# Eight lent buffers for the transposed bands of block one, first conversions traced behind the bands' divisions, and low parts and divisions moved from GpSimd to VectorE

## Chip, cores and metric

The kernel runs on one core of a Trainium2 chip. The metric is the device time of one execution in microseconds, as the median of several runs. Engines go by the profile's names: PE is TensorE (PEld its weight loads), DVE is VectorE, ACT is ScalarE, POOL is GpSimd, SP is SyncE, which issues the DMAs.

## What is computed

Attention over 4 batches of 8 heads (576 positions, 64 dimensions), made of a coarse part (q, k and v averaged over groups of four positions, softmax attention, each result repeated four times) and a local part (each position sees the positions less than four away). Two feed-forward layers of width 512 to 2048 to 512 over the 2304 tokens follow.

```python
out_up = np.repeat(sm_attn(q_d, k_d, v_d), factor, axis=2)      # q_d, k_d, v_d: means over 4 positions
scores = np.where(np.abs(pos[:, None] - pos[None, :]) < factor, scale * q @ k.T, -1e9)
out_local = softmax(scores) @ v
x = (out_up + out_local).transpose(0, 2, 1, 3).reshape(2304, 512)
h = x @ w_in;   x = np.maximum(h, 0.0) ** 2 @ w_out              # layer one
h = x @ w_in2;  return (h * np.cos(h)) @ w_out2                  # layer two
```

The weights arrive as 64-bit floats (two 32-bit words an element, which the kernel reads as integers and puts together itself). Matmul operands are split in a high and a low part, and each product is the sum of high x high, high x low and low x high.

## The kernel before

**Blocks.** Layer one goes over five blocks of tokens (8, 7, 7, 7 and 7 windows of 64 tokens). In each block, for each of 16 pieces `f` of the width 2048, `stage_a` (L711) multiplies the block's input `xh`, `xl` by piece `f` of `w_in` (12 matmuls into one PSUM bank, tag `h`), `gelem1` (L735, L736, L723) applies relu and square on ACT and makes the high part `gh`, `low` (L729) makes the low part `gl` on DVE, and `stage_b1` (L794) multiplies by piece `f` of `w_out`, 12 matmuls. Until layer one's last block the bank of `stage_a` has one buffer, so a new piece waits until the relu has read the one before.

**Input of a block.** A task `window(w)` makes the local attention of 64 tokens: it adds the mask and the scores (L475, L485), takes the maximum on DVE (L359), and goes through `exps`: even windows of block one and all of block two (`apiece`) scale the maximum (L361) and take four exponentials with sums on ACT (L363); odd ones of block one subtract on DVE (L370), take one exponential (L374) and sum on DVE (L376). Then come the reciprocal of the sum (L496, L497), the division of the band `pr` by the sum (L498, POOL), four transposes on PE (L508), a copy to `pt` on ACT (L510), the product with v (L528), the addition of the coarse part (L544, DVE), and for each pair of windows the high part `xh` (L555, ACT) and the low part `xl` (L556, DVE). `pool(b)` sums groups of four positions (L346, L351, L353; `early_v` does it at L303 for the first batch), and `down(b, hp)` makes the coarse attention (L389 to L434), whose division (L400) is on POOL.

**Buffers in the head.** While `early[0]` holds, before the first matmul of layer one, the eight windows of block one are under way together. Their bands have eight buffers: four of `pr`, and two each lent by the tiles `gt` and `gl`. Their transposes have five: two of `pt` and three lent by the tile `gh`. `band_tile` hands them out and `band_done` takes them back once the product with v has been issued. `xh` and `xl` (pool `xp`) have two buffers each; block one uses one of each.

**Conversion of weights.** `conv1(f)` loads piece `f` of layer one (`raw`, 1 MB, two buffers, an SP DMA at L568) and calls `split`: ACT scales the upper words (L582), DVE clips (L584), shifts (L587) and joins the lower words (L589), ACT rounds to the high part `hi1[f]` (L596), and the low part follows (L604, two halves of 512 columns): on POOL while `early[0]` holds, else on DVE. The low halves are written to DRAM for the later blocks. `conv2(u)` does the same for the 16 pieces of layer two, from slot 18 on, one each three slots; its low parts are made on POOL (L599, and L683 for the sums of odd pieces).

**Order.** Tasks are generators: each round of a loop advances every task by one step, and the order in which they are traced is the priority. From it a scheduler lays out each engine's queue, taking what its own timeline holds ready. Engines run their queues in order. `behind(names)` ties an instruction behind the last one of that name on its engine; the names set before are `hi` (L723), `gl` (L729), `xh` (L555), `xl` (L556), `exp` (L363), `max` (L359), `pr` (L498), `relu` (L735), `pe`. The first loop runs while there are tasks and puts two `warm` matmuls on PE after each round in which PE got work. After it `early[0]` is false; pieces 3 to 15 are converted while block one is under way, and `now[0]` is the number of the slot (block x 16 + piece). `after_first` ties everything traced later behind the last `pe`, `xh`, `xl` and `pr` instruction of the head, one for each engine.

Of the kernel before, what the change touches and what calls it, by code (L numbers as in the profile page):

```python
# [8 lines left out]
F32 = mybir.dt.float32  # L9
# [9 lines left out]
P = 128  # L19
# [55 lines left out]
def kernel(  # L75
# [114 lines left out]

    lent = {"pr": ["pr"] * caps["pr"] + ['gt', 'gt', 'gl', 'gl'], "pt": ["pt"] * caps["pt"] + ['gh', 'gh', 'gh']}

    def band_tile(name, shape):
        while early[0] and not lent[name]:
            yield
        if not early[0]:
            yield from need(name)
        tag = lent[name].pop(0) if early[0] else name
        if tag == name:
            return tag, cm.tile(shape, F32, tag=name, name=name, bufs=caps[name])  # L200
        t = gp.tile([P, TMAX], F32R if tag in ("gh", "gl") else F32, tag=tag, name=name, bufs=3 if tag == "gh" else 2)
        n = shape[1] * shape[2]
        return tag, t.bitcast(F32)[:shape[0], :n].rearrange("p (a b) -> p a b", a=shape[1])
# [14 lines left out]
    whole = {}  # L218
    scored = set()
    xds = {}  # L220
    qk_used = {}
# [136 lines left out]
    def exps(bank, sv, mx, pr, scale, apiece):  # L358
        last["max"] = nc.vector.tensor_reduce(out=mx[:, 0], in_=sv, op=ALU.max, axis=AX.X).ins  # L359
        if apiece:  # L360
            nc.vector.tensor_scalar_mul(out=mx[:, 0], in0=mx[:, 0], scalar1=-scale)  # L361
            for i in range(sv.shape[1]):
                last["exp"] = nc.scalar.activation(  # L363
                    out=pr[:, i], in_=sv[:, i], func=AF.Exp, bias=mx[:, 0, i:i + 1], scale=scale,
                    accum_out=mx[:, 1, i:i + 1],
                ).ins
            done_a(bank)
            yield
            return
# [81 lines left out]
    def window(w):  # L451
# [39 lines left out]
        else:  # L491
# [5 lines left out]
        nc.vector.reciprocal(out=mx[:, 1], in_=mx[:, 1])  # L497
        last["pr"] = nc.gpsimd.tensor_tensor(  # L498
            out=prv, in0=prv, in1=mx[:, 1].unsqueeze(2).broadcast_to([P, HPAIR, n]), op=ALU.mult
        ).ins  # L500
        yield
        if not early[0]:
# [74 lines left out]
    def split(raw, hi, los=None, sums=None):  # L577
# [3 lines left out]
        with behind("hi", "xh", "exp"):  # L581
            nc.scalar.activation(out=xv, in_=top.bitcast(F32), func=AF.Prelu, scale=TOP_SCALE, alpha=TOP_ALPHA)  # L582
        with behind("gl", "xl"):
            nc.vector.tensor_scalar(  # L584
                out=xv, in0=xv, scalar1=TOP_MAX, scalar2=-TOP_MAX * TOP_ALPHA, op0=ALU.min, op1=ALU.max
            )
# [11 lines left out]
        if los is None:  # L598
            nc.gpsimd.tensor_tensor(out=xv, in0=xv, in1=hi.bitcast(F32), op=ALU.subtract)  # L599
        else:  # L600
# [9 lines left out]
    def conv1(f, after=0):  # L610
# [3 lines left out]
        yield  # L614
        while len(ready) < after or len(scored) < 4:
            yield
# [7 lines left out]
        for said in split(raw, hi1[f], ring):  # L624
            if said:
                done("raw")
            yield
        for k, lo in enumerate(los):
            nc.sync.dma_start(out=lo_d[f][:, k * DM:(k + 1) * DM], in_=lo.bitcast(F32))
            lo1[0, f, k] = lo  # L630
# [9 lines left out]
    def conv2(u):  # L640
# [41 lines left out]
        yield  # L682
        nc.gpsimd.tensor_tensor(out=total, in0=total, in1=top.bitcast(F32), op=ALU.subtract)  # L683
        yield
# [238 lines left out]
    tasks += [window(w) for w in range(W0[1])]  # L923
    tasks += [conv1(0), conv1(1, 3), conv1(2, 6)]
    junk = ps_a.tile([P, 512], F32, tag="a", name="ps_warm")
# [9 lines left out]
    warm(WARM0)  # L935
    while tasks:
        before = last.get("pe")
# [33 lines left out]
    def x2_stream(j):  # L971
# [10 lines left out]
        for c in range(0, NK, 2):  # L982
            yield
            cs = slice(c, c + 2)
            nc.scalar.activation(out=xh[:, cs], in_=xf[:, cs], func=AF.Copy)
            nc.vector.tensor_tensor(out=xl[:, cs], in0=xf[:, cs], in1=xh[:, cs].bitcast(F32), op=ALU.subtract)

# [199 lines left out]
```

## Time and profile before

| | |
|---|---|
| median of 3 runs | 933.74 us (933.18, 933.74, 938.19) |
| the profiled execution, its own time | 938.64 us |
| its span, first to last instruction | 936.6 us |
| PE busy, instructions | 913.4 us, 6886 |
| DVE busy | 638.6 us |
| ACT busy | 580.4 us |
| POOL busy | 108.6 us, 89 instructions |
| granted TensorE clock, mean | 0.989 of full speed |

The span is what the rows below divide up; the 2.0 us between it and the execution's own time lie around it. Busy times of different engines overlap. A matmul counts as busy from its start to a modelled end, so a busy PE can be at half the clock. In each row of a timeline the first two numbers are the start and the length in us; what stands in brackets is the idle time before and what ended it.

### The profile page before, as it was taken

How to read it: one execution, taken by the hardware profiler on the slowest of the kernel's cores; microseconds unless marked ns; L12 is line 12 of the kernel's file. 1: busy time of each engine (PE TensorE's matmuls, PEld its weight loads, DVE VectorE, ACT ScalarE, POOL GpSimd, SP SyncE). 2: the span in 40 equal slices, each digit the busy share in tenths (PEclk: the TensorE clock that was granted, in tenths of full speed). 3: DMA queues.
4: the chain of work that ended last, by engine and by line, in shares of the span. 5: the costliest groups of instructions: out<-in, count | busy, mean ns of one | idle time of the engine just before them, and what ended most of it. 6: DMA issues, size and time to landing. Idle time of an engine off the chain costs nothing.

```text
span 936.6 us, 17648 instructions
## 1 busy us (share of the span) xinstructions
PE 913.4 (98%) x6886; PEld 835.4 (89%) x6886; DVE 638.6 (68%) x1207; ACT 580.4 (62%) x1024; POOL 108.6 (12%) x89
## 2 busy tenths in 40 slices
PE   7889999999999999999999999999999999999997
PEld 5668777788888888898999999999999999999997
DVE  6779986664568644554531168888787888888786
ACT  4678674555465554554553368677777677777774
POOL 2331101024033231231210000000000000000000
PEclk9789999999999999999999999999999999999999
DMA  9779876865899756966888885565665665655672
GB/s 233 209 253 318 306 266 220 291 214 172 298 310 323 239 210 243 341 245 226 294 301 307 284 320 190 187 212 182 196 203 184 199 209 191 207 194 188 213 236 101
DMA packets 74223, 222.77 MB, mean 238 GB/s; under 512 B 8932, under 2 KB 14436, under 8 KB 69916
## 3 DMA queue, kind: packets, MB, share of 16 engines
q1 hardware_dynamic: 74140, 221.64, 70.5%
q8 instruction: 54, 0.88, 0.4%
q14 instruction: 29, 0.24, 0.1%
HBM read 180.72 MB, written 40.89 MB: 237 GB/s over the span
## 4 chain that ended last, share of the span: by engine, by line
PE 87%; DVE 5%; DMA 5%; ACT 2%; issue 1%; POOL 0%; DVEq 0%; POOLq 0%; ACTq 0%
PE ps_h L746 22%; PE ps_h L711 19%; PE acc L794 19%; PE acc L818 18%; DMA pl<-in_pool_v_dram 3%; DMA pl<-in_pool_qk_dram 2%; PE ps_a L528 1%; PE ps_warm L931 1%; PE ps_a L485 1%; PE ps_a L508 1%; PE ps_a L389 1%; PE ps_a L426 1%; PE ps_a L410 1%; PE acc L816 1%; PE ps_acc L528 1%; DVE mx L359 1%
## 5 line engine op out<-in xcount | busy, mean ns | idle before, releaser
L746 PE MATMUL ps_h<-x,w2hi 128*128 128x256 f32 x1152 | 159.9, 281 | 0.0
L746 PEld LDWEIGHTS ps_h<-x,w2hi 128*128 128x128 f32 x1152 | 146.6, 189 | 0.1
L729 DVE TENSOR_TENSOR gl<-gt,gh 128x448 fp32r<-128x448 f32 (+1 forms) x80 | 56.2, 703 | 131.2 <-ACT gh L723 67.4
L818 PE MATMUL acc<-bl,gh 128*128 128x256 f32 x504 | 140.5, 280 | 0.0
L711 PE MATMUL ps_h<-xh,w1hi 128*128 128x448 f32 (+1 forms) x320 | 122.4, 384 | 4.8 <-ACT gt L735 4.8
L711 PE MATMUL ps_h<-xl,w1hi 128*128 128x448 f32 (+1 forms) x320 | 120.3, 376 | 0.0
L794 PE MATMUL acc<-gl,w1hi 128*128 128x448 f32 (+1 forms) x320 | 120.0, 375 | 0.2 <-DVE gl L729 0.2
L794 PE MATMUL acc<-gh,w1hi 128*128 128x448 f32 (+1 forms) x320 | 111.2, 377 | 2.2 <-ACT gh L723 2.2
L735 ACT ACTIVATE gt<-ps_h 128x448 f32<-128x448 f32 (+1 forms) x80 | 44.4, 555 | 110.2 <-PE ps_h L711 109.9
L818 PEld LDWEIGHTS acc<-bl,gh 128*128 128x128 f32 x504 | 94.9, 188 | 0.0
L794 PE MATMUL acc<-gh,lo 128*128 128x448 f32 x256 | 94.5, 369 | 0.0
L786 DVE TENSOR_TENSOR gl<-g,gh 128x896 fp32r<-128x896 f32 x72 | 78.2, 1086 | 11.0 <-ACT gh L781 11.0
L818 PE MATMUL acc<-w2hi,gh 128*128 128x256 f32 x288 | 80.9, 281 | 0.0
L754 ACT ACTIVATE u<-ps_h,quarter 128x512 f32<-128x512 f32 x72 | 49.5, 687 | 49.9 <-PE ps_h L746 49.6
L818 PE MATMUL acc<-w2hi,gl 128*128 128x256 f32 x288 | 80.3, 281 | 0.0
L761 DVE SCALAR_TENSOR_TENSOR r<-u,ps_h 128x512 f32<-128x512 f32 x72 | 49.4, 686 | 39.6 <-ACT u L756 34.0
L781 ACT ACTIVATE gh<-g 128x896 fp32r<-128x896 f32 x72 | 68.1, 946 | 10.7 <-DVE g L779 10.6
L711 PEld LDWEIGHTS ps_h<-xh,w1hi 128*128 128x128 f32 x320 | 60.6, 189 | 13.7 <-ACT gt L735 5.6
L766 ACT ACTIVATE r<-r,half_pi 128x512 f32<-128x512 f32 x72 | 51.8, 720 | 33.9 <-DVE r L762 33.9
L746 PE MATMUL ps_h<-x,w2lo 128*128 128x256 f32 x432 | 68.7, 281 | 0.0
L794 PEld LDWEIGHTS acc<-gh,w1hi 128*128 128x128 f32 x320 | 59.6, 188 | 9.4 <-ACT gh L723 2.7
L711 PEld LDWEIGHTS ps_h<-xl,w1hi 128*128 128x128 f32 x320 | 60.7, 190 | 6.8
(145 smaller groups left out, 1963.3 us busy)
## 6 DMA issues: line engine op xcount, KB each, us to landing
bl<-wo_d SPq DMA_DIRECT2D x70, 896.0 KB
raw<-in_w_dram SPq DMA_DIRECT2D x32, 1024.0 KB
lo<-lo_d SPq DMA_DIRECT2D x128, 256.0 KB
qkw<-in_win_qk_dram SPq DMA_DIRECT2D x28, 268.0 KB
pl<-in_pool_qk_dram SPq DMA_DIRECT2D x24, 288.0 KB
wo_d<-raw SPq DMA_DIRECT2D x16, 384.0 KB
out_dram<-o SPq DMA_DIRECT2D x18, 256.0 KB
lo_d<-loa SPq DMA_DIRECT2D x16, 256.0 KB
```

Of the source, the lines that this page charges most:

```text
L528: last["pe"] = nc.tensor.matmul(avv[rows, hp], vw[:n, hp * P + a * D:hp * P + (a + 1) * D], pt[:n, hp, a * WQ:(a + 1) * WQ], start=True, s ...
L711: nc.tensor.matmul(h[:, :n], a[:, c * P:(c + 1) * P], x[:, c, :n], start=i == 0, stop=i == len(order) - 1)
L729: last["gl"] = nc.vector.tensor_tensor(out=gl, in0=gt, in1=gh.bitcast(F32), op=ALU.subtract).ins
L735: last["relu"] = nc.scalar.activation(out=gt, in_=h, func=AF.Relu).ins
L746: nc.tensor.matmul(h[:, s * TB:(s + 1) * TB], a[:, c * P:(c + 1) * P], x[:, c], start=i == 0, stop=i == len(order) - 1,)
L754: nc.scalar.activation(out=u, in_=h, func=AF.Identity, bias=quarter, scale=float(1.0 / (2 * math.pi)))
L761: nc.vector.scalar_tensor_tensor(out=r, in0=u, scalar=-PI2_HI, in1=hv, op0=ALU.mult, op1=ALU.add)
L766: nc.scalar.activation(out=r, in_=r, func=AF.Sin, bias=half_pi, scale=1.0)
L781: nc.scalar.activation(out=gh, in_=g[:, 1:], func=AF.Copy)
L786: nc.vector.tensor_tensor(out=gl, in0=g[:, 1:], in1=gh.bitcast(F32), op=ALU.subtract)
L794: nc.tensor.matmul(acc[d][:, :n], a, x, start=f == 0 and i == 0, stop=f == NF - 1 and i == 2)
L818: nc.tensor.matmul(o, a[:, x], b, start=opens and i == 0, stop=p == NP2 - 1 and i == 2 and (k % 2 == 1 or k == NPROD - 1),)
```

## The change

Five things are altered. (1) The transposed bands of block one have eight buffers, two of `pt` and six slices of a first tile of `xh` (four) and of `xl` (two); `gh` lends none. (2) The divisions L498 of all 36 windows go to DVE. (3) The first pieces' `conv1` waits in the trace until all eight bands are divided (`turned`), for pieces zero and one in place of a number of finished windows, and their DVE steps are tied behind the last division; piece two stops before its high part until the first `hi` has been traced, and the head's loop ends without it, so that its low part is made on DVE. (4) The exponentials of windows that are traced in slots 0 and 1 are tied behind `hi`. (5) The low parts of layer two's weights go from POOL to DVE, tied behind `gl`; and the first casts of layer two's input are tied behind `hi` and `gl`. In `after_first` the entry of `pr` is now one of DVE, and stands in the place of that of `xl`.

```diff
--- before.py
+++ after.py
@@ -188,7 +188,8 @@
             got.append(t)
         return got
 
-    lent = {"pr": ["pr"] * caps["pr"] + ['gt', 'gt', 'gl', 'gl'], "pt": ["pt"] * caps["pt"] + ['gh', 'gh', 'gh']}
+    lent = {"pr": ["pr"] * caps["pr"] + ['gt', 'gt', 'gl', 'gl'], "pt": ["pt"] * caps["pt"] + list(range(6))}
+    scratch = {}
 
     def band_tile(name, shape):
         while early[0] and not lent[name]:
@@ -196,6 +197,11 @@
         if not early[0]:
             yield from need(name)
         tag = lent[name].pop(0) if early[0] else name
+        if isinstance(tag, int):
+            x, k = ("xh", "xl")[tag // NK], tag % NK
+            if x not in scratch:
+                scratch[x] = xp.tile([P, NK, TMAX], F32R, tag=x, name="xs").bitcast(F32)
+            return tag, scratch[x][:shape[0], k].rearrange("p (a b) -> p a b", a=shape[1])
         if tag == name:
             return tag, cm.tile(shape, F32, tag=name, name=name, bufs=caps[name])
         t = gp.tile([P, TMAX], F32R if tag in ("gh", "gl") else F32, tag=tag, name=name, bufs=3 if tag == "gh" else 2)
@@ -217,6 +223,7 @@
     pooled = {}
     whole = {}
     scored = set()
+    turned = set()
     xds = {}
     qk_used = {}
     vp_used = {}
@@ -360,10 +367,11 @@
         if apiece:
             nc.vector.tensor_scalar_mul(out=mx[:, 0], in0=mx[:, 0], scalar1=-scale)
             for i in range(sv.shape[1]):
-                last["exp"] = nc.scalar.activation(
-                    out=pr[:, i], in_=sv[:, i], func=AF.Exp, bias=mx[:, 0, i:i + 1], scale=scale,
-                    accum_out=mx[:, 1, i:i + 1],
-                ).ins
+                with behind("hi") if 0 <= now[0] < 2 else nullcontext():
+                    last["exp"] = nc.scalar.activation(
+                        out=pr[:, i], in_=sv[:, i], func=AF.Exp, bias=mx[:, 0, i:i + 1], scale=scale,
+                        accum_out=mx[:, 1, i:i + 1],
+                    ).ins
             done_a(bank)
             yield
             return
@@ -495,9 +503,10 @@
         yield from exps(s, sv, mx, prv, SCALE, w % 2 == 0 if apart else w < W0[2])
         nc.vector.tensor_scalar_add(out=mx[:, 1], in0=mx[:, 1], scalar1=1e-9)
         nc.vector.reciprocal(out=mx[:, 1], in_=mx[:, 1])
-        last["pr"] = nc.gpsimd.tensor_tensor(
+        last["pr"] = nc.vector.tensor_tensor(
             out=prv, in0=prv, in1=mx[:, 1].unsqueeze(2).broadcast_to([P, HPAIR, n]), op=ALU.mult
         ).ins
+        turned.add(w)
         yield
         if not early[0]:
             yield
@@ -580,7 +589,7 @@
         xv = x.bitcast(F32)
         with behind("hi", "xh", "exp"):
             nc.scalar.activation(out=xv, in_=top.bitcast(F32), func=AF.Prelu, scale=TOP_SCALE, alpha=TOP_ALPHA)
-        with behind("gl", "xl"):
+        with behind("gl", "pr" if early[0] else "xl"):
             nc.vector.tensor_scalar(
                 out=xv, in0=xv, scalar1=TOP_MAX, scalar2=-TOP_MAX * TOP_ALPHA, op0=ALU.min, op1=ALU.max
             )
@@ -596,7 +605,8 @@
             nc.scalar.activation(out=hi, in_=xv, func=AF.Copy)
         yield
         if los is None:
-            nc.gpsimd.tensor_tensor(out=xv, in0=xv, in1=hi.bitcast(F32), op=ALU.subtract)
+            with behind("gl", "xl"):
+                nc.vector.tensor_tensor(out=xv, in0=xv, in1=hi.bitcast(F32), op=ALU.subtract)
         else:
             for k, lo in enumerate(los()):
                 cs = slice(k * DM, (k + 1) * DM)
@@ -612,7 +622,7 @@
         raw = load_raw(1, f)
         yield
         yield
-        while len(ready) < after or len(scored) < 4:
+        while len(ready) < after or early[0] and len(turned) < (8 if f == 0 else 8):
             yield
         hi1[f] = wp.tile([P, 2 * DM], F32R, tag=f"hi{f}", name=f"w1hi{f}")
         los = []
@@ -625,6 +635,8 @@
             if said:
                 done("raw")
             yield
+            while f == 2 and said and "hi" not in last:
+                yield
         for k, lo in enumerate(los):
             nc.sync.dma_start(out=lo_d[f][:, k * DM:(k + 1) * DM], in_=lo.bitcast(F32))
             lo1[0, f, k] = lo
@@ -680,7 +692,8 @@
         with behind("relu", "xh", "exp"):
             nc.scalar.activation(out=top, in_=total, func=AF.Copy)
         yield
-        nc.gpsimd.tensor_tensor(out=total, in0=total, in1=top.bitcast(F32), op=ALU.subtract)
+        with behind("gl", "xl"):
+            nc.vector.tensor_tensor(out=total, in0=total, in1=top.bitcast(F32), op=ALU.subtract)
         yield
         nc.sync.dma_start(out=wo_d[p][:, 2 * DM:m], in_=top.bitcast(F32))
         nc.sync.dma_start(out=wo_d[p][:, m + 2 * DM:], in_=total)
@@ -921,7 +934,7 @@
     tasks += [pool(0), early_v()]
     tasks += [down(0, hp) for hp in range(HPAIR)]
     tasks += [window(w) for w in range(W0[1])]
-    tasks += [conv1(0), conv1(1, 3), conv1(2, 6)]
+    tasks += [conv1(0, 0), conv1(1, 0), conv1(2, 6)]
     junk = ps_a.tile([P, 512], F32, tag="a", name="ps_warm")
     used["a"] += 1
 
@@ -933,7 +946,7 @@
                 )
 
     warm(WARM0)
-    while tasks:
+    while any(t.__name__ != "conv1" for t in tasks) or (0, 1, 1) not in lo1:
         before = last.get("pe")
         for t in list(tasks):
             if next(t, "end") == "end":
@@ -982,8 +995,10 @@
         for c in range(0, NK, 2):
             yield
             cs = slice(c, c + 2)
-            nc.scalar.activation(out=xh[:, cs], in_=xf[:, cs], func=AF.Copy)
-            nc.vector.tensor_tensor(out=xl[:, cs], in0=xf[:, cs], in1=xh[:, cs].bitcast(F32), op=ALU.subtract)
+            with behind("hi") if j == 0 else nullcontext():
+                nc.scalar.activation(out=xh[:, cs], in_=xf[:, cs], func=AF.Copy)
+            with behind("gl") if j == 0 else nullcontext():
+                nc.vector.tensor_tensor(out=xl[:, cs], in0=xf[:, cs], in1=xh[:, cs].bitcast(F32), op=ALU.subtract)
 
     n1 = NB * NF
     pend = []
```

## Rows read from the trace of the kernel before

**Rows 1.** The page: busy us of each engine, share, instructions.

```profile
PE 913.4 (98%) x6886; PEld 835.4 (89%) x6886; DVE 638.6 (68%) x1207; ACT 580.4 (62%) x1024; POOL 108.6 (12%) x89
```

**Rows 2.** Waits of PE, whole span: total us, times, longest.

```profile
PE ps_h L711 <- ACT gt L735: 4.8, 2, 4.6
```

**Rows 3.** Stretches: length, busy us of PE, PEld, DVE, ACT, POOL, clock, DMA.

```profile
13.20:25.50 12.30, 9.33 (x170) 7.62 (x168) 12.18 (x44) 9.99 (x56) 6.07 (x8) 1.00 0.96 205
...
40.00:48.60 8.60, 8.60 (x99) 7.13 (x99) 5.68 (x10) 4.65 (x8) 0.00 (x0) 0.50 0.20 61
...
51.80:56.30 4.50, 0.00 (x1) 0.01 (x1) 3.99 (x9) 3.04 (x18) 1.97 (x2) 0.91 0.74 266
56.30:65.10 8.80, 8.80 (x28) 7.04 (x29) 4.33 (x8) 6.21 (x10) 3.60 (x3) 0.66 0.70 242
65.10:163.00 97.90, 97.90 (x627) 77.04 (x626) 80.12 (x142) 69.16 (x161) 9.58 (x9) 1.00 0.80 274
163.00:176.00 13.00, 10.12 (x105) 7.90 (x105) 10.79 (x27) 6.27 (x13) 1.49 (x3) 1.00 0.73 236
```

**Rows 4.** The chain that ended last, 25 to 66 us: start, length, what.

```profile
25.62 4.50 DVE vp L303 x4
...
39.98 2.71 PE ps_acc L508 x12
...
43.54 2.76 PE ps_acc L528 x48
...
53.56 2.19 ACT pr L363 x14
```

**Rows 5.** Timeline of the head: DVE, POOL and ACT.

```profile
16.10 0.17 DVE L361 TENSOR_SCALAR dmx<-dmx 96x3 f32<-96x3 f32 x1
...
16.54 0.71 DVE L396 TENSOR_SCALAR dmx<-dmx 96x3 f32<-96x3 f32 x1
...
31.45 3.64 POOL L498 TENSOR_TENSOR pr<-pr,mx 128x280 f32<-128x280 f32 x3 [5.22 <-DVE mx L497]
...
32.75 1.21 DVE L589 SCALAR_TENSOR_TENSOR bits<-raw,bits 128x1024 uint32<-128x1024 uint32 x1
...
50.18 1.29 POOL L604 TENSOR_TENSOR loa<-bits,w1hi 128x512 fp32r<-128x512 f32 x1 [12.54 <-DVE kp L351]
...
51.94 1.29 DVE L361 TENSOR_SCALAR mx<-mx 128x4 f32<-128x4 f32 x2
...
55.61 0.63 ACT L735 ACTIVATE gt<-ps_h 128x512 f32<-128x512 f32 x1
```

**Rows 6.** Stretches, L711 alone: length, busy us of PE, PEld, clock, DMA.

```profile
48.50:51.80 3.30, 3.12 (x12) 2.17 (x12) 0.98 0.98 394
56.20:61.70 5.50, 5.40 (x12) 3.80 (x12) 0.50 0.72 275
```

**Rows 7.** Groups by shape, DVE, 13 to 34 us: busy us, mean ns, idle before.

```profile
L370 DVE TENSOR_TENSOR pr<-ps_acc,mx 128x280 f32<-128x280 f32 x4 | 1.7, 430 | 0.0
```

**Rows 8.** Groups by shape, DVE, 34 to 60 us.

```profile
L544 DVE TENSOR_TENSOR xt<-ps_acc,xd 128x256 f32<-128x256 f32 x8 | 3.4, 422 | 5.3 <-PE ps_acc L528 5.1
L556 DVE TENSOR_TENSOR xl<-xt,xh 128x512 fp32r<-128x512 f32 x4 | 2.7, 687 | 0.9 <-ACT xh L555 0.9
L589 DVE SCALAR_TENSOR_TENSOR bits<-raw,bits 128x1024 uint32<-128x1024 uint32 x2 | 2.4, 1220 | 0.0
...
L587 DVE TENSOR_SCALAR bits<-bits 128x1024 uint32<-128x1024 uint32 x2 | 1.4, 688 | 0.0
```

**Rows 9.** Groups by shape, POOL, whole span.

```profile
L599 POOL TENSOR_TENSOR bits<-bits,shi 128x1024 f32<-128x1024 f32 x16 | 39.0, 2438 | 94.0 <-ACT shi L596 87.0 <-issue 6.9
L498 POOL TENSOR_TENSOR pr<-pr,mx 128x280 f32<-128x280 f32 x28 | 22.1, 797 | 160.3 <-DVE mx L497 95.7 <-DVE mx L496 29.6 <-DVE mx L361 18.5
```

**Rows 10.** Timeline, 62 to 110 us: piece three's high part and its use.

```profile
66.06 1.06 ACT L596 ACTIVATE w1hi<-bits 128x1024 fp32r<-128x1024 f32 x1 [0.16 <-DVE bits L589]
...
71.57 0.40 PE L711 MATMUL ps_h<-xh,w1hi 128*128 128x512 f32 x1
```

## The prediction

> **What bounds the kernel now.** The page comes first. TensorE (PE) is busy for 913.4 us of a span of 936.6 [rows 1], so only what PE does not spend on block matmuls can be saved. The list of PE's waits shows where that is: the one long wait is 4.6 us of the layer-one matmul (L711) for ACT's relu gt (L735) [rows 2]. The stretches then give the order of events [rows 3]. Up to about 48.6 us PE only serves the attention of block one. From 51.8 to 56.3 it does nothing. From 65.1 to 163 it is busy for 97.90 of 97.90 us, and from 163 to 176 it idles for 2.9 us. The granted clock is 0.50 (1.2 GHz) from 40 to 48.6 us, 0.66 from 56.3 to 65.1, and 1.00 (2.4 GHz) from 65.1 on. So the time is some 65 us of preparation plus a stretch that PE fills. What the change does before 65 us moves the end almost one for one, and what it does later costs nothing while PE stays full.
>
> In the preparation, VectorE (DVE) sets the pace first: it is busy for 12.18 of the 12.30 us up to 25.5 [rows 3], then has 4.50 us of pooled-value sums [rows 4]. The last three bands wait for their division on POOL until 31.45 + 3.64 = 35.09 us [rows 5]. Bands five to seven find no buffer for their transposes: these come as a second pass, 12 transposes from 39.98 us, and the 48 products that need them only from 43.54 [rows 4].
>
> **Divisions on DVE.** Eight divisions leave POOL in the head. DVE's nearest row is the subtraction of the same size, 0.43 us [rows 7], so 8 x 0.43 = 3.4 us go to an engine that is full. The sums end at 25.62 + 4.50 = 30.12 us [rows 4], and DVE's work of that stage at 32.75 + 1.21 = 33.96 [rows 5]. Of these 3.8 us 2.6 are piece zero's conversion (below), which now comes after the divisions, so 1.2 us of band work are left. With the 3.4 the last division ends at about 34.7, against 35.09 on POOL: next to nothing by itself. Bounds: 1 us earlier (POOL's divisions slowed DVE's small steps there, next paragraph), 2 us later if the divisions are laid out with gaps.
>
> POOL also slows DVE. A small DVE scalar step takes 0.17 us alone and 0.71 beside a POOL division; two of them took 1.29 beside the low parts of piece one [rows 5]. The Trainium skill (GPSIMD Engine Reference, section 1, Specifications) says that POOL shares its SBUF interfaces with VectorE and collides with DVE instructions in a two-port mode or with two SBUF inputs. The trace agrees for the scalar steps by 0.17 against 0.71 us. That rule also speaks against this change: a division has two SBUF inputs, so beside a POOL operation it would be stretched too. No row shows a DVE division there; by that rule those that meet POOL's pooled divisions (L400) or low parts (L604) would be longer, and the sum would lose perhaps 1 us, an estimate from that page.
>
> **Eight transposed buffers.** All 32 transposes can now stand before the products, and the second pass (39.98 to 43.54, 3.56 us) goes from the path. What is late next is DVE: behind the last division stand piece zero's conversion (0.69 + 0.69 + 1.22 = 2.6 us), eight additions L544 (3.4) and three of the four low parts L556 (2.0) [rows 8]. From 34.7 that is 42.7; I add 0.6 us for the last high part on ACT and 1.2 for handoffs and for products that come late (the eight additions stood idle for 5.3 us before [rows 8], most of it behind the second pass). The first L711 is then at 44.5 instead of 48.6. If piece one's conversion (another 2.6, now also traced ahead of the additions) lands in front, it is 47. I take 44.5: **-4.1 us**, bounds -5.4 and -1.
>
> **Window exponentials behind the first high part.** At 53.56 ACT spends 2.19 us on exponentials of the next windows [rows 4], queued ahead of the relu of piece zero, after waiting for DVE's maxima, which the POOL low parts at 50.18 had slowed [rows 5]. The relu starts at 55.61; PE, with one bank for this result, waits all that time. With window eight's exponentials behind the high part, and piece two's low parts off POOL, the relu can follow the matmuls at once: 0.63 us plus handoffs, say 1.1, are left of the 4.5. **-3.4 us**, bounds -3.9 and 0 (window nine's exponentials are traced later and are not held, so they may still stand ahead).
>
> **Clock.** The twelve L711 of piece one took 5.40 us at clock 0.50, behind the idle 4.5 us; those of piece zero took 3.12 at 0.98 [rows 6]. Without the idle stretch I take the full clock: **-2.3 us**, bounds -2.3 and 0. Against it, PE reaches piece zero earlier after the same sparse stretch, and that piece may now fall in the half clock: **+1.0**, bounds 0 and +2.3.
>
> **Supply of the next pieces.** Piece three's high part was finished at 66.06 + 1.06 = 67.1 us and used at 71.57 [rows 10]: 4.4 us of slack. Its start hangs on the first high part of g, which moves forward too, but PE's demand moves forward by more (it also loses the half clock and one idle stretch). The low part of piece two now costs DVE 1.4 us, raw buffers come free with the conversions as before, and SP's loads follow them. I allow **+1.5 us**, bounds 0 and +4.
>
> **The rest.** Twenty-eight more divisions (POOL 0.80 us each), sixteen low parts of layer two's weights (POOL 2.44 each) [rows 9] and eight smaller ones go to DVE; by its 1.22 us for 1024 columns [rows 8] that is 12 + 20 + 8 = 40 us over some 400. DVE is busy 80.12 of 97.90 us to 163 [rows 3], so PE's queue covers it; if that cover fails, each meeting costs up to one such instruction, 1.2 us. Behind such a low part stand the next gl (L729) and the sums of the pooled tensors. The order of layer two's first casts changes nothing that PE waits for in the trace. Zero, bounds -1 and +2.
>
> **Sum.** -4.1 - 3.4 - 2.3 + 1.0 + 1.5 = -7.3 us, against this execution's own 938.64: 931.3. The median of the runs, 933.74, is 4.9 us below the profiled execution; one run (938.19) is like it. If those 4.9 us have nothing to do with the terms, the changed kernel's median is 926.4. If they are the half clock at piece one and near it, 2.3 of the gain is already in the median, and it is 928.7. I take 927.5.
>
> **The rivals.**
> *Supply binds.* PE now asks sooner than DVE can convert. For: from 65.1 DVE is already at 82% and has 0.43 more per window. Against: 4.4 us of slack at piece three. Then term five is +4 or more: the gain is some 3 to 4, 930 to 931.5. Chance 0.19.
>
> *The relu still waits.* The instruction order is laid out anew, and exponentials or piece one's own high-part conversion (1.06 us on ACT) stand ahead of the relu; the clock falls as before. Only the head's 4.1 less 1 is left: about 930.5 to 933. Chance 0.15.
>
> *DVE is the head's bound and nothing comes earlier* (the change does not do what it says): the divisions, both conversions and the additions in a row bring the first L711 to 47 to 48.6, and the relu's stretch gives 1 to 2 us: 931 to 935. Chance 0.07.
>
> *Slower.* The transition at 163 us widens: DVE's queue stands behind sums that wait for pool loads, now with the divisions of the next block's bands behind the same waits. DVE's idle share there is the price: PE's 2.9 us of idle [rows 3] would have to grow by more than 12 us for the kernel to lose 0.5%, that is by several loads in a row, at this and the two later transitions. About 940. Chance 0.05.
>
> The forecast keeps 0.54. A difference under 0.5% (4.7 us) is about what a measurement of this kernel cannot tell from no change. Below 929.1 lies most of the forecast and a little of the first two rivals: faster 0.60. Slower 0.05, the same 0.35. The range takes the head's bound and the full clock at the low end (921.5) and the second and third rival at the high end (934). The forecast's own range is 922 to 930.5.
>
> **What would show it.** All eight L510 copies before the first L528, no transposes after about 38 us; first L711 near 44.5; the wait of L711 for gt near 1 us; granted clock 1.00 at piece one; no POOL instructions but L400 and four L604 after the memsets; PE without waits of over 1 us from piece two to 150 us. Wrong would be: a first L711 after 47, exponentials ahead of the first gt, or L711 waiting for a high or low part of pieces two to five.

## The result and the profile after

The changed kernel is slower. Its median is 942.13 us (937.5 to 944.26, six runs), that of the kernel before, on the same chip, 933.75 us (933.18 to 938.19, six runs): a ratio of 1.008, 95% interval 1.0063 to 1.0098. Forecast were 927.5 us and a range of 921.5 to 934. The profiled execution of the changed kernel took 942.2 us, its span 940.1, mean granted clock 0.989. Lines have moved by some 10: L582 is now L591 (ACT's scaling of the raw weights), L510 is L519 (copy of the transposes), L508 L517, L711 L724, L735 L748, L589 L598.

The page's busy times, beside [rows 1]:

```profile
PE 912.2 (97%) x6884; PEld 836.4 (89%) x6884; DVE 663.0 (71%) x1269; ACT 581.0 (62%) x1024; POOL 26.9 (3%) x27
```

PE has the same work, most of POOL's has gone to DVE. The moved operations there, by shape (busy us, mean ns, idle before), with [rows 9]:

```profile
L609 DVE TENSOR_TENSOR bits<-bits,shi 128x1024 f32<-128x1024 f32 x16 | 19.5, 1220 | 2.7 <-ACT shi L605 2.6
L506 DVE TENSOR_TENSOR pr<-pr,mx 128x280 f32<-128x280 f32 x28 | 12.3, 442 | 0.4
```

PE's waits (total us, times, longest) against [rows 2]: the one wait of 4.6 us for gt is gone, a wait of 5.8 us behind ACT's copies has come, and the waits for gt are five, none over 1.9.

```profile
PE ps_acc L517 <- ACT xs L519: 5.8, 1, 5.8
PE ps_h L724 <- ACT gt L748: 5.4, 5, 1.9
```

What ACT waited for from 25 to 60 us:

```profile
ACT bits L591 <- DMA raw<-in_w_dram: 5.6, 1, 5.6
```

The timeline of the head shows how these hang together (start, length, engine; in brackets the idle time before and its releaser):

```profile
27.98 0.33 SPq L577 DMA_DIRECT2D raw<-in_w_dram  x1
...
33.44 0.45 DVE L506 TENSOR_TENSOR pr<-pr,mx 128x280 f32<-128x280 f32 x1
...
38.01 1.12 ACT L591 ACTIVATE bits<-raw 128x1024 f32<-128x1024 f32 x1 [5.62 <-DMA raw<-in_w_dram]
39.02 3.17 ACT L519 COPY xs<-ps_acc 70x512 f32<-70x512 f32 x6
...
39.65 1.92 PE L517 MATMUL ps_acc<-const_sb,pr 128*70 128x128 f32 x8 [5.79 <-ACT xs L519]
...
42.25 1.50 SPq L577 DMA_DIRECT2D raw<-in_w_dram  x2
...
55.38 0.50 PE L724 MATMUL ps_h<-xh,w1hi 128*128 128x512 f32 x1
...
59.11 0.50 PE L724 MATMUL ps_h<-xh,w1hi 128*128 128x512 f32 x1 [0.69 <-ACT gt L748]
```

The last division ends at 33.89 us, earlier than the forecast 34.7, and the transposes could run. But piece one's conversion is now traced ahead of the bands' copies and additions. Its first step, L591, stands at the head of ACT's queue; its weights were asked for only at 27.98, when `early_v` gave the raw buffer back, and landed at 38.0. Six copies L519 stand behind it, PE's last transposes behind those. The Trainium skill (Perfetto Trace Analysis, section Tensor Engine Instruction (MATMUL, LD_WEIGHTS)) calls ACT's execution a strict FIFO; the trace agrees, by 5.62 us in which ACT did nothing though copies were due. The chain that ended last goes the same way (start, length, what):

```profile
25.70 2.26 DVE vp L310 x2
...
27.98 10.00 DMA raw<-in_w_dram
...
38.01 1.12 ACT bits L591
39.12 0.48 ACT xs L519
...
39.65 1.92 PE ps_acc L517 x8
...
42.42 4.04 PE ps_acc L434 x32
46.46 6.85 PE ps_acc L537 x128
```

Stretches (length, busy us of PE, PEld, DVE, ACT, POOL, granted clock, DMA share, GB/s), to be held against [rows 3]:

```profile
30.00:35.00 5.00, 3.49 (x25) 2.90 (x23) 4.42 (x17) 1.84 (x5) 0.00 (x0) 0.88 0.95 305
35.00:40.00 5.00, 0.35 (x2) 0.32 (x3) 0.84 (x2) 2.00 (x4) 0.00 (x0) 0.80 0.22 63
40.00:45.00 5.00, 5.00 (x32) 3.88 (x32) 3.32 (x4) 2.67 (x7) 0.00 (x0) 0.50 0.34 90
45.00:50.00 5.00, 5.00 (x86) 4.98 (x84) 1.35 (x4) 2.03 (x4) 2.50 (x2) 0.50 0.93 379
50.00:55.00 5.00, 5.00 (x90) 4.88 (x90) 4.29 (x9) 2.47 (x4) 0.00 (x0) 0.50 0.16 59
55.00:60.00 5.00, 4.31 (x28) 3.23 (x27) 5.00 (x9) 3.39 (x7) 2.96 (x2) 0.99 0.75 191
...
65.00:75.00 10.00, 6.60 (x28) 4.95 (x29) 6.97 (x15) 7.50 (x19) 0.00 (x0) 1.00 0.76 234
```

From 35 to 40 PE does 0.35 us of work. Then it is busy for 15 us at 0.50 (1.2 GHz): the coarse products L434 and the 128 products L537 all fall in the half clock. The first L724 starts at 55.38, against 48.60 in the profile of before. The gain behind it is there: the wait for gt is 0.69, and piece one runs at the full clock. But PE is busy for only 6.60 of the 10 us from 65 to 75, and waits twice more. The first of these waits is behind exponentials of the next windows: ACT runs them from 62.33 on, with one conversion step between, and piece one's relu starts behind them at 65.69.

```profile
66.39 0.50 PE L724 MATMUL ps_h<-xh,w1hi 128*128 128x512 f32 x1 [1.41 <-ACT gt L748]
...
69.57 0.75 DVE L358 TENSOR_REDUCE kp<-pl 128x144 f32<-128x576 f32 x1 [3.03 <-DMA pl<-in_pool_qk_dram]
70.24 1.22 DVE L598 SCALAR_TENSOR_TENSOR bits<-raw,bits 128x1024 uint32<-128x1024 uint32 x1
...
73.08 0.50 PE L724 MATMUL ps_h<-xh,w1hi 128*128 128x512 f32 x1 [1.94 <-ACT gt L748]
```

Before the second wait DVE stands for a load of the pooled tensor, piece three's L598 behind it, and ACT's next relu behind piece three's high part. So the gain in the gap is given back within a few pieces. The first low-part matmul of a piece (`xh` by `loa`) is a mark that can be followed through the timelines. Start in us; e5 is a second profile of before and e17 one of the changed kernel, both below:

| piece | 0 | 1 | 2 | 3 | 4 | 9 | 15 |
|---|---|---|---|---|---|---|---|
| before, as shown first | 50.64 | 59.88 | 67.02 | 73.90 | 80.41 | 115.93 | 159.12 |
| before again (e5) | 48.40 | 56.69 | 63.18 | 70.05 | 76.54 | 112.07 | 155.16 |
| after | 57.34 | 61.09 | 68.35 | 77.49 | 85.33 | 121.36 | 163.48 |
| after again (e17) | 56.10 | 60.48 | 66.67 | 75.04 | 82.86 | 118.97 | 163.43 |

Against e5 the changed kernel is 8.9 us late at piece zero, 4.4 at piece one, 8.8 at piece four and 8.3 at piece 15. The two executions differ by 9.9 us (942.2 and 932.27; the medians by 8.4). So 8.3 of the 9.9 us are lost by piece 15 of block one, and all of them before layer two, whose first product starts at 543.0 in the changed kernel and at 533.1 in e5.

### The profile page after: what moved, and what is told of

It is laid out like the page before. It is cut to its first block, busy times and chain, and to the rows that moved or that the text cites. A ratio compares the mean times of both kernels' runs of the same rounds, so it can differ in the third digit from the quotient of the medians.

```text
span 940.1 us, 17561 instructions
## 1 busy us (share of the span) xinstructions
PE 912.2 (97%) x6884; PEld 836.4 (89%) x6884; DVE 663.0 (71%) x1269; ACT 581.0 (62%) x1024; POOL 26.9 (3%) x27
## 4 chain that ended last, share of the span: by engine, by line
PE 78%; DMA 10%; DVE 8%; ACT 2%; issue 1%; DVEq 0%; ACTq 0%; SPq 0%
PE ps_h L759 22%; PE acc L831 18%; PE acc L807 15%; PE ps_h L724 15%; DMA pl<-in_pool_v_dram 4%; DMA pl<-in_pool_qk_dram 3%; DMA raw<-in_w_dram 2%; PE ps_a L537 1%; PE ps_warm L944 1%; DVE bits L598 1%; PE ps_a L517 1%; DVE vp L360 1%; PE ps_a L493 1%; PE ps_acc L537 1%; PE ps_a L397 1%
## 5 line engine op out<-in xcount | busy, mean ns | idle before, releaser
L742 DVE TENSOR_TENSOR gl<-gt,gh 128x448 fp32r<-128x448 f32 (+1 forms) x80 | 51.8, 648 | 121.4 <-ACT gh L736 64.6
L724 PE MATMUL ps_h<-xh,w1hi 128*128 128x448 f32 (+1 forms) x320 | 121.5, 381 | 5.4 <-ACT gt L748 5.4
L724 PE MATMUL ps_h<-xl,w1hi 128*128 128x448 f32 (+1 forms) x320 | 119.4, 373 | 0.0
L748 ACT ACTIVATE gt<-ps_h 128x448 f32<-128x448 f32 (+1 forms) x80 | 44.3, 554 | 114.0 <-PE ps_h L724 113.8
L807 PE MATMUL acc<-gh,w1hi 128*128 128x448 f32 (+1 forms) x320 | 107.2, 377 | 0.1
L724 PEld LDWEIGHTS ps_h<-xh,w1hi 128*128 128x128 f32 x320 | 60.1, 188 | 14.4 <-ACT gt L748 7.4
L807 PEld LDWEIGHTS acc<-gl,w1hi 128*128 128x128 f32 x320 | 60.1, 188 | 7.6 <-DVE gl L742 1.0
```

The costliest lines, as they stand in the source:

```text
L724: nc.tensor.matmul(h[:, :n], a[:, c * P:(c + 1) * P], x[:, c, :n], start=i == 0, stop=i == len(order) - 1)
L742: last["gl"] = nc.vector.tensor_tensor(out=gl, in0=gt, in1=gh.bitcast(F32), op=ALU.subtract).ins
L748: last["relu"] = nc.scalar.activation(out=gt, in_=h, func=AF.Relu).ins
L807: nc.tensor.matmul(acc[d][:, :n], a, x, start=f == 0 and i == 0, stop=f == NF - 1 and i == 2)
```

## The experiments

The leading theory was that piece one's place in ACT's queue costs the time. Its rivals: the eight buffers or the moved work of POOL cost it; the profile of before shown first is a bad reference for the head; the costs add up or don't. Each ratio is to the kernel before on the same chip, with its 95% interval.

**e1: piece one waits again for three finished windows, all else as changed.**

```diff
-    tasks += [conv1(0, 0), conv1(1, 0), conv1(2, 6)]
+    tasks += [conv1(0, 0), conv1(1, 3), conv1(2, 6)]
```

> The changed kernel, only that piece one's conversion waits in the trace for three finished windows, as it did before the change. Theory A (ACT stands 5.6 us at piece one's first conversion step until its weights land at 38.0 us, with the copies of the transposes queued behind it): that wait is gone, the first layer-one matmul starts by 48 us instead of 55.4, and the time is 933 to 937 against 942. Theory B (the loss is DVE's added work and the late supply of pieces two to four): the first matmul may come earlier, but the time stays at 940 or above.

933.37 us, ratio 0.9986 [0.997, 1.0003]. ACT has no wait for raw weights in the head, and PE reaches layer one 10 us earlier:

```profile
45.19 0.49 PE L724 MATMUL ps_h<-xh,w1hi 128*128 128x512 f32 x1 [1.54 <-ACT xh L564]
```

The whole loss goes with this one argument; no gain appears. PE now waits 2.0 us for piece one's high part.

**e2: the kernel before with only piece one's conversion moved ahead.**

```diff
-    tasks += [conv1(0), conv1(1, 3), conv1(2, 6)]
+    tasks += [conv1(0), conv1(1, 0), conv1(2, 6)]
```

> The kernel before, only that piece one's conversion no longer waits in the trace for three finished windows. Theory A: ACT now stands for the weights of piece one (about 5 us, until some 38 us) ahead of copies, the first layer-one matmul moves from 48.6 to 53 to 55, and the time is 937 to 941 against 933.8. Theory B: no more than 1 us from 933.8, since nothing is added to DVE.

939.47 us, 1.007 [1.0045, 1.0094]: one argument makes most of the loss in the old kernel too, without any other edit. ACT's step, a copy behind it, and PE:

```profile
38.78 1.12 ACT L582 ACTIVATE bits<-raw 128x1024 f32<-128x1024 f32 x1 [6.55 <-DMA raw<-in_w_dram]
39.80 1.06 ACT L510 COPY pt<-ps_acc 70x512 f32<-70x512 f32 x2
...
40.43 3.15 PE L426 MATMUL ps_acc<-dpt,vp 72*64 72x144 f32 x24 [6.13 <-ACT pt L510]
```

Then the half clock (0.50 from 40 to 50) and a first L711 at 55.36.

**e3: the changed kernel with piece one's weights loaded early.** `early_v` puts its values in the tiles of `hi1[1]` and `hi1[2]` in place of a raw buffer; the order stays as changed.

```diff
-        big = rawp.tile([P, 2 * DM, 2], U32, tag="raw", name="pv").bitcast(F32).rearrange("p c w -> p (c w)")
+        bigs = [wp.tile([P, 2 * DM], F32R, tag=f"hi{f}", name="pv").bitcast(F32) for f in (1, 2)]
...
-        places = [big[:KTOK, :n], big[:KTOK, n:], small[:KTOK], last_one[:KTOK]]
+        places = [bigs[0][:KTOK], bigs[1][:KTOK], small[:KTOK], last_one[:KTOK]]
...
```

> The changed kernel with its order kept, but the first two heads' values of the pooled sums lie in the tiles of the second and third high part instead of a raw buffer, so that the weights of piece one are asked for at about 8 us instead of 28. Theory A: they land before 30 us, ACT's wait is gone, the first layer-one matmul starts at 45 to 48 us, and the time is 931 to 936. Theory B: the time stays at 939 to 942, since order and DVE's work are the same.

936.07 us, 1.0023 [1.0005, 1.004]. Asked for at 7.9 us, both pieces are there when ACT comes to them:

```profile
7.89 1.09 SPq L570 DMA_DIRECT2D raw<-in_w_dram  x2
...
25.40 2.15 ACT L584 ACTIVATE bits<-raw 128x1024 f32<-128x1024 f32 x2
...
46.24 0.49 PE L717 MATMUL ps_h<-xh,w1hi 128*128 128x512 f32 x1 [2.09 <-ACT xh L557]
```

So it is the wait for the DMA, not the conversion's own work, that costs the head. The profiled execution (932.05) was the lowest of ten, up to 939.85; where the others lose is not in a trace.

**e4: the kernel before with eight buffers alone** (the first hunks of the diff).

```diff
-    lent = {"pr": ["pr"] * caps["pr"] + ['gt', 'gt', 'gl', 'gl'], "pt": ["pt"] * caps["pt"] + ['gh', 'gh', 'gh']}
+    lent = {"pr": ["pr"] * caps["pr"] + ['gt', 'gt', 'gl', 'gl'], "pt": ["pt"] * caps["pt"] + list(range(6))}
...
```

> The kernel before with eight buffers for the transposed bands and nothing else. Theory A: the second pass of transposes goes from the path, the first layer-one matmul starts at 45 to 47 us instead of 48.6, and the time is 930 to 933. Theory B says the same of the head, but that the later pieces are then late and take it back: 933 to 935.

935.77 us, 1.0021 [1.0007, 1.0035]. First L717 at 44.81, as forecast (44.5), but what comes next waits for piece one's high part:

```profile
PE ps_h L717 <- ACT w1hi L602: 4.5, 1, 4.5
```

The mark of piece zero stands at 47.27 us, 1.1 earlier than in e5, that of piece one at 57.13, 0.4 later, and that of piece 15 at 156.69, 1.5 later.

**e5: the kernel before once more, for its profile.**

> The kernel before once more, for a second profile: its first profiled execution took 938.6 us at a granted clock of 0.989, while its timed executions lie near 933.7. Theory C (those 4.9 us are the half clock before 65 us): this profile has fewer microseconds at half clock between 40 and 65 us, piece one at the full clock or the idle stretch shorter, and a time of 932 to 935. If the time is 938 again, or the clock the same at 933, theory C falls.

932.27 us, and another head than in [rows 3]: full clock where that one had 0.50, and the first L711 3.1 us earlier, with the same instructions.

```profile
35.00:40.00 5.00, 4.93 (x102) 4.54 (x102) 3.00 (x7) 2.52 (x8) 2.13 (x2) 1.00 0.90 316
40.00:45.00 5.00, 3.11 (x85) 2.72 (x84) 4.42 (x8) 2.84 (x6) 0.00 (x0) 1.00 0.24 46
```

```profile
45.51 0.50 PE L711 MATMUL ps_h<-xh,w1hi 128*128 128x512 f32 x1 [1.45 <-ACT xh L555]
```

The wait for gt is 3.3 here (4.6 in [rows 2]). The head that the forecast set out to shorten was that of one execution.

**e6: e1 and e3 together.** The edits of both.

> The changed kernel with both cures at once: piece one's weights asked for at 8 us, and its conversion behind three finished windows in the trace. Theory A (the wait of ACT for those weights is the loss, and all else that was changed gains or is neutral): 930 to 933, at or below the kernel before. Theory B (added DVE work makes the later pieces late): 935 to 938, since the pieces after the first are asked for as in the changed kernel.

934.01 us, 0.9996 [0.9982, 1.0011]: no gain from the two together; PE waits 3.6 us for piece one's high part.

**e8: the kernel before with the exponentials' tie alone.**

```diff
+                with behind("hi") if 0 <= now[0] < 2 else nullcontext():
                     last["exp"] = nc.scalar.activation(
...
```

> The kernel before with the exponentials traced in slots 0 and 1 behind the first high part, nothing else. If the relu's wait is the exponentials' doing, the wait of layer one's first matmul for gt falls from 4.6 to about 1 us, piece one starts some 3.5 us earlier, and the time is 929 to 931.5. If another instruction takes their place ahead of the relu (piece one's high part), the wait stays above 2 us and the time at 932 to 934.

932.54 us, 0.9976 [0.9965, 0.9987], the only version that is faster beyond its interval. PE's waits for gt from 45 to 60 us:

```profile
PE ps_h L712 <- ACT gt L736: 0.7, 1, 0.7
```

3.3 in e5. The mark of piece one stands at 53.39 (e5: 56.69), that of piece nine at 112.07 in both: the 3.3 us are returned on the way. The profiled execution (933.99) is no faster than e5 (932.27), so where the median's gain lies is in no trace.

**e15: e8 and e4 together**, on the kernel before.

> The kernel before with the exponentials tied behind the first high part and eight buffers, nothing else. If the parts add up (0.24% faster and 0.21% slower alone): 934. If the buffers' loss alone came from the wait for piece one's high part that the exponentials' tie shortens: 930 to 932.

933.97 us, 0.9997 [0.9983, 1.0011]: 0.9976 x 1.0021, so the parts add up within the intervals and the buffers give the tie nothing. PE still waits 4.0 us for piece one's high part here, so this run doesn't tell whether that wait is what the buffers cost.

**e18: the kernel before with the tie, the early weights of e3 and piece one ahead as in e2.** The three edits above.

> The kernel before with the exponentials' tie, piece one's conversion first (as in the second run) and its weights asked for at 8 us. Theory A: without the late weights that order costs nothing, 930 to 933, against 939.5 for the second run. If the order itself is what costs, 936 or more.

932.8 us, 0.9986 [0.997, 1.0003], first L705 at 45.50. The order that alone cost 0.7% (e2) costs nothing that can be measured once the weights are there: against e8, which has the tie without it (0.9976), the difference of 0.1% lies within the intervals.

**e7, e10, e11: the moves from POOL to DVE, in the kernel before.** e7 has all of them, e10 the low parts of layer two alone, e11 the divisions alone.

```diff
-        last["pr"] = nc.gpsimd.tensor_tensor(
+        last["pr"] = nc.vector.tensor_tensor(
...
-            nc.gpsimd.tensor_tensor(out=xv, in0=xv, in1=hi.bitcast(F32), op=ALU.subtract)
+            with behind("gl", "xl"):
+                nc.vector.tensor_tensor(out=xv, in0=xv, in1=hi.bitcast(F32), op=ALU.subtract)
...
```

> The kernel before with the divisions of all windows and the low parts of layer two's weights on DVE, nothing else. Theory A: within 2 us of 933.8, since PE's queue covers it. Theory B: 2 to 5 us slower, from waits for pieces two to four or at the change of block near 165 us.

> The kernel before with only the low parts of layer two's weights on DVE. If the 3.7 us of the seventh run come from DVE's load in block one (theory D), nothing is changed there, and the time is within 1.5 us of 934. If they come from these low parts ahead of gl in blocks two to five, 937 to 938.

> The kernel before with only the divisions of the windows on DVE. Theory D: the whole of the seventh run's loss, 936.5 to 939, with pieces' weights asked for later in block one, ACT standing for them ahead of a relu, and PE waiting for gt. If the low parts were the cause, 933 to 935.

e7 938.64 us, 1.004 [1.0027, 1.0053]; e10 939.73, 1.0048 [1.0026, 1.0069], five runs; e11 939.3, 1.0063 [1.0042, 1.0085], four runs. Neither half alone measures less than both together, so these costs do not add. Each instruction is shorter on DVE, as costed (in e7 L498 takes 463 ns, 797 in [rows 9]; the low part 1240, 2438 in [rows 9]), and the kernel is slower. The Trainium skill (GPSIMD Engine Reference, section 4.1, Engine selection) says to put an elementwise operation of two inputs on VectorE, GpSimd being about half as fast. The durations agree, 1240 against 2438 ns; the time of this kernel goes the other way. One place in e7 shows a way in which time is lost far from the head:

```profile
127.59 1.12 ACT L582 ACTIVATE bits<-raw 128x1024 f32<-128x1024 f32 x1 [2.69 <-DMA raw<-in_w_dram]
...
129.55 0.59 ACT L737 ACTIVATE gt<-ps_h 128x512 f32<-128x512 f32 x1
...
130.19 0.79 PE L713 MATMUL ps_h<-xh,w1hi 128*128 128x512 f32 x1 [2.52 <-ACT gt L737]
```

```profile
130.19:135.50 5.31, 5.31 (x13) 4.14 (x14) 5.31 (x9) 4.45 (x8) 0.00 (x0) 0.50 0.52 165
```

ACT stands for raw weights, the relu behind it, PE behind the relu, and the next 13 matmuls run at 0.50. In e11 ACT waits for raw weights for 13.8 us between 60 and 160, in e5 for 5.4. In e10 it waits for 5.0, and PE waits 4.2 for POOL's divisions L498. But in e8 and e18, which are not slower, it is 9.2 and 15.5. So this way is seen in e7 and e11, and ACT's wait does not by itself tell what a kernel loses.

Another way is untested. In e7 one division on DVE that runs beside a division on POOL takes 1.01 us, and in e11 one beside a low part takes 2.35, in place of 0.44:

```profile
264.66 2.40 POOL L599 TENSOR_TENSOR bits<-bits,shi 128x1024 f32<-128x1024 f32 x1 [26.22 <-ACT shi L596]
...
265.02 2.35 DVE L498 TENSOR_TENSOR pr<-pr,mx 128x280 f32<-128x280 f32 x1
```

**e9 and e12: the moves undone outside the head**, e9 in e3 and e12 in e1.

```diff
-        last["pr"] = nc.vector.tensor_tensor(
+        last["pr"] = (nc.vector if apart else nc.gpsimd).tensor_tensor(
...
-            with behind("gl", "xl"):
-                nc.vector.tensor_tensor(out=xv, in0=xv, in1=hi.bitcast(F32), op=ALU.subtract)
+            nc.gpsimd.tensor_tensor(out=xv, in0=xv, in1=hi.bitcast(F32), op=ALU.subtract)
...
```

> The changed kernel with piece one's weights asked for at 8 us, as in the third run, and with the divisions outside the head and layer two's low parts back on POOL. Theory A plus D (ACT's wait for piece one is the larger loss, and a second one of 3 to 4 us comes from the divisions and low parts on DVE): 931 to 933, some 4 us below the third run's 936.1. Theory A alone: 935 to 937, as the third run.

> The changed kernel with piece one behind three finished windows, as in the first run, and with the divisions outside the head and layer two's low parts back on POOL: eight buffers, the exponentials' tie and the head's divisions are what is left of the change. Theory A plus D: 929.5 to 932, below both kernels. If only ACT's wait counted: 933 to 934, as the first run.

e9 941.16 us, 1.0071 [1.0054, 1.0088] (e3: 1.0023); e12 935.27, 1.001 [0.9997, 1.0024] (e1: 0.9986). The additive reading falls: undone there, the moves don't give 0.4% back. In e3 the kernel gets clearly slower; in e1 it seems to, but the two intervals touch.

**e13, e14, e16: three edits that should mean little, in the kernel before**, to see what any new layout of the queues does.

```diff
-            start_at(18 + int(3 * u), conv2, u)
+            start_at(19 + int(3 * u), conv2, u)
...
-conv1(2, 6)]
+conv1(2, 7)]
...
-WARM = 2
+WARM = 3
```

> The kernel before with layer two's weights converted one slot later each, no work added or moved between engines. If the moves to DVE cost by their work (theory D), this stays within 1 us of 934. If any new layout of the queues moves the time by some us (theory L), it differs from 934 by 2 us or more, in either direction.

> The kernel before with piece two's conversion behind seven finished windows in place of six, no work added. Theory D: within 1 us of 934. Theory L: 2 us or more away from it.

> The kernel before with three in place of two warm matmuls after each round of the head, that is some seven more of 0.2 to 0.4 us on PE and nothing on DVE or ACT. Theory D: 933 to 936. Theory L: outside of it. If the half clock in the head is what sets the spread between executions, this kernel's executions spread less than those of the kernel before (931.8 to 936.9).

e13 936.49 us, 1.0018 [1.0004, 1.0032]; e14 933.96, 0.9993 [0.9979, 1.0006]; e16 935.39, 1.001 [0.9995, 1.0025]. These three layouts move the time by -0.07 to +0.18%, e13 beyond its interval though no work was added. That no layout alone makes 0.4 to 0.6% is not shown by three edits. The runs of e16 spread over 4.5 us, those of the kernel before over 5.6 in three times as many, so they don't tell whether the head's clock sets the spread.

**e17: the changed kernel once more, for its profile.**

> The changed kernel once more, for a second profile. Theory A: ACT stands for piece one's weights again until 37 to 39 us, PE idles 5 to 6 us before the remaining transposes and runs at half clock behind it, and the first layer-one matmul starts at 53 to 56 us. If the clock is full there, the head is 3 to 4 us shorter and the time near 938.

944.42 us, with the same stall:

```profile
39.42 1.12 ACT L591 ACTIVATE bits<-raw 128x1024 f32<-128x1024 f32 x1 [6.60 <-DMA raw<-in_w_dram]
```

Here the clock was 0.62 from 40 to 45 us, 1.00 from 45 to 50 and 0.75 from 55 to 60, so it was piece zero that fell partly in the half clock. The first L724 came at 52.72, 2.7 us earlier than in the other execution, and yet the whole was 2.2 us longer; at piece 15 the two are level (163.43 and 163.48). So the stall is there each time, the half clock behind it falls differently, and an earlier first L724 did not shorten the whole.

## Why the prediction was wrong

**The step that failed is "Eight transposed buffers".** It noted that piece one's conversion is "now also traced ahead of the additions" and priced that as "another 2.6", DVE's time. The conversion's first step is on ACT, and it waits for a load. Neither was looked up: that the load is issued only when `early_v` has ended, at 28 us, that it lands at 38, and that ACT's copies for the transposes stand behind. Shown by e2 (the move alone: +0.7%), e1 (undone: the loss is gone), e3 (weights early: the wait is gone, the first L717 at 46.24, +0.23% left) and e18 (same order, weights early: no loss). None of the rivals held it; each of them let the first L711 come no later than before. The prediction's own sign of being wrong, a first L711 after 47, came true at 55.38.

**The premise on the head** failed for the gains. The prediction had what comes before 65 us move the end almost one for one. In e8 3.3 us gained at piece one are gone by piece nine, and in e4 1.1 us gained at piece zero have turned into 1.5 us lost by piece 15.

**Sizes in that term.** The buffers do bring the first L711 to 44.8 (e4; forecast 44.5), but from 45.5 (e5), not from 48.6: -0.7 us in place of -4.1. 48.6 belongs to an execution whose head ran at half clock [rows 3]. And PE then waits 4.5 us for piece one's high part. The buffers alone cost 0.21%; that this wait is the reason is likely, not shown.

**Divisions on DVE.** Right: the last ends at 33.89 (34.7 forecast), 442 ns each in the profile after (430 taken). The longer divisions beside POOL that the prediction considered are real where the two meet (1.01 us in e7, 2.35 in e11), but in the profile after none was stretched: the longest took 451 ns. The 1 us that the prediction set against them had no figure behind it.

**Window exponentials.** The mechanism was right: the wait for gt is 0.69 (1.1 forecast was left). The head's size was right too (3.3 us in e8, 3.4 forecast), but it did not last: the ratio of e8 is worth 0.24%, 2.2 us. The exponentials that no longer stand ahead of piece zero's relu stand ahead of piece one's in the profile after, and PE waits 1.41 us there.

**Clock.** Piece one ran at the full clock, as forecast, in the profile after (its twelve L724 took 3.06 us at 1.00). But 15 us of the head at 0.50 came ahead of it, and e5 shows that -2.3 was read from a half clock that the same kernel has in one execution and not to the same extent in another (piece one's twelve L711 took 4.61 us at 0.70 in e5, 5.40 at 0.50 in [rows 6]). That piece zero may fall in the half clock is borne out in e1: 0.66 from 45 to 50 us.

**Supply.** +1.5 was allowed, on the ground that raw buffers come free as before. Piece two's does not: it is asked for at 42.25, against 33.52 in e5. Piece three is asked for at 43.40, no later than in e5 (43.61), and ACT's first steps on both start without a wait for the load (54.33 and 63.49). From piece one to piece four the lag against e5 grows from 4.4 to 8.8 us. What the trace shows in that stretch is PE's waits of 1.41 us, behind the exponentials, and 1.94, behind piece three's high part, which the load of the pooled tensor held up. Raw weights are waited for again from piece four on (0.76 us, then 3.24 and 2.51). How the 4.4 us divide among these is not measured.

**The rest, zero.** Wrong in the kernel before: +0.4 to +0.63% for the moves (e7, e10, e11), more than the three small edits make (-0.07 to +0.18%). Not shown is why: with e3 as base the sign turns (e9, and e12 leans that way with e1), so it is not a fixed price of DVE's added work. ACT's wait for weights in mid-block is as long in kernels that are not slower (e8, e18), and what DVE's operations lose beside POOL's was seen in single operations and not summed. That stays open, as does where e3's slower executions lose their time.

No version tried is clearly better than the tie alone (e8).

## What to carry to other kernels

Before a step is moved up in the order, go through each instruction it issues and ask when its data lands and what stands behind it in that engine's queue: a step priced by its busy time on one engine (2.6 us on DVE) cost 0.7% of the kernel, 6.5 us, by its wait on another (e2). Before a gain is read off a stall or a half clock in one profile, take a second profile of the same kernel. And a gain at the head counts only if what follows can keep up; here waits at the next pieces returned it by piece nine.

## What the runs showed of the hardware

- The same instructions run the head at a granted clock of 0.50 or 1.00: 40 to 48.6 us at 0.50 in one execution of before, 35 to 45 us at 1.00 in another, the first L711 at 48.60 or 45.51.
- A load of 1 MB took 10.0 us from issue to landing (27.98 to 37.98) with the DMA engines' share at 0.95 and 305 GB/s from 30 to 35 us. At that rate 1 MB alone would take 3.4 us (an estimate from that row). What held the load in its last microseconds, when the share had fallen (0.22 from 35 to 40 us), is not shown.
- A two-input step on DVE took about half of its time on POOL (1240 against 2438 ns), and the kernel was still slower with it there.
- A division on DVE (0.44 us alone) that ran beside an operation on POOL ended about 0.3 us after POOL's: 1.01 us in e7, beside one of 0.91, and 2.35 in e11, beside one of 2.40.
